# Values behind scores from step 45, and the first keys and queries turned by TensorE: a change to a fused top-k attention and tanh-shrink kernel

## The chip, the cores and the metric

The kernel runs on one core of a Trainium2 chip. Five engines work side by side, each through its own instructions in order: TensorE (PE; its weight loads are listed as PEld), VectorE (DVE), ScalarE (ACT), GpSimd (POOL) and SyncE (SP), which here only issues transfers. Transfers run on 16 DMA engines. The metric is the device time of one launch in microseconds (us).

## The reference

All is float32 except the weights of the second block, which arrive as float64. Eight batches, eight heads, 576 rows, head size 64; then a block over 4608 tokens with 512 features and 2048 hidden ones.

```python
scores = scale * np.matmul(q, k.transpose(0, 1, 3, 2))            # B, H, 576, 576
kth = np.partition(scores, -32, axis=-1)[..., -32:-31]
scores = np.where(scores >= kth, scores, -1000000000.0)
attn = np.exp(scores - np.max(scores, axis=-1, keepdims=True))
attn = attn / (np.sum(attn, axis=-1, keepdims=True) + 1e-09)
x = np.matmul(attn, v)                                            # heads joined: 4608 x 512
h = x @ w_in                                                      # 4608 x 2048
out = (h - np.tanh(h)) @ w_out                                    # 4608 x 512
```

## The kernel before

**Steps.** The work is cut into 144 steps, numbered n in the code and here. A step is 128 query rows (a query tile, `qt` 0 to 3) of a pair of heads (`hp` 0 to 3) of a batch, with all 576 keys; the two heads lie in the two halves of the partitions. Each batch has 16 such steps, and two more (`rem`) that take the last 64 rows of two pairs together. Batch 0 is steps 0 to 17.

**What a step does.** `scores` multiplies queries and keys on PE into one PSUM bank set (`scps`, one buffer) and copies them to SBUF on ACT (`sc`, L244). `search` finds the 32 largest per row on DVE: a minimum and a maximum of the two halves of the keys (L266, L267, the last reads of `scps` by DVE), then four rounds of MAX8 (L274) and three of MATCH_REPLACE8 (L277). Between the rounds stand other DVE jobs: `between(i)` runs what is put down for round i. `mask` builds the threshold on POOL (L293), applies a steep Relu on ACT (L306) and subtracts on POOL, one head after the other (L309). `expo` takes the exponential on ACT (L329). Then the probabilities have to be turned so that keys lie on partitions: in batch 0 by PE against an identity matrix (`turn_pe`, L423, a bank `zt` of two buffers, copied out by ACT, L426), later by DVE in 32x32 blocks (`turn_z`, L386) and two hops of DMA through DRAM (`spread_keys`, L401 and L403). `values` multiplies them with v on PE (L451, the same two-buffer bank, tile `av`) and copies the product to `xT` on ACT (L471); from batch 1 on it comes five steps behind its search.

**The second block.** When all pairs of a unit of 256 (in batch 0 sometimes 128) rows are done, `values` appends the unit's matmuls to the list `work`: L502 into `hps` (evicted by tanh and copy on ACT, L514 and L515, and subtracted on POOL, L516), then L523 into `ops` (copied by ACT, L533, and sent out by SP, L535). `rate` sets a share of that list for each step, and `deal` issues it in parts: 0.4 of a step's share ahead of the scores, 0.6 behind. These are FFN matmuls below.

**The order is written out by hand.** One loop over n issues everything, and each engine runs its instructions in that order. In a step it is: transposes of batch 0's probabilities, `mask(n-1)`, `search(n)`, `spread_keys`, `deal`, `scores(n+1)`, `expo(n-1)`, `deal`, loads, `deal`. `due` issues the values of a step five back. Up to step 44 it stands at the head of the loop; from `NEAR = 45` on it stands between the first `deal` and `scores(n+1)`.

**The start.** All rows of batch 0 are asked for at once, ahead of step 0, with the weights between them, on SP's queue. `load_rows` brings k or q of a pair of heads as four transfers of 32 partitions with runs of 32 floats (128 bytes), so that `turn_rows` can turn them by 32x32 blocks on DVE (L221). Pairs 1 to 3 of batch 0 land in room that later belongs to the weights `w_in[2]` and `w_in[3]` (`early`). Their turns are put down for round 0 of steps 0, 1 and 2: pair 1 in step 0, and so on. The weights are made float32 in 32 pieces of 128 x 512 during steps 0 to 10 (`convert`): two transfers (L148, L149), then DVE (L157, L162), ACT (L160, L165), DVE (L168) and POOL (L171). Pieces 0 to 3 wait behind one load of k and q each in SP's queue. After its last load, v is brought by `load_v` (L211: 128 KB in runs of 256 bytes, L215: 16 KB).

Of the kernel before, what the change touches and what calls it, by code (L numbers as in the profile page):

```python
# [10 lines left out]
FP32 = mybir.dt.float32  # L11
# [8 lines left out]
J = 4  # L20
# [31 lines left out]
def kernel(  # L52
# [9 lines left out]
    nc = tc.nc  # L62
    P = nc.NUM_PARTITIONS
    B, H, S, D = q.shape
    DM, DFF = moe_w_in.shape
    NHP = H // 2
    JP = J * P
    R = S - JP
# [16 lines left out]
    def pool(name, bufs, **kw):  # L85
        return ctx.enter_context(tc.tile_pool(name=name, bufs=bufs, **kw))
# [14 lines left out]
    zt_ps = pool("zt_ps", 2, space=PS)  # L101
    h_ps = pool("h_ps", 2, space=PS)

    ident = consts.tile([P, P], FP32, name="ident")
# [3 lines left out]
    w_in = [consts.tile([P, CD, DFF // WJ], FP32, name=f"w_in{j}") for j in range(WJ)]  # L108
# [14 lines left out]
    def flat(x):  # L123
        return x.rearrange("p n w -> p (n w)")
# [51 lines left out]
    raw, kT, qT, vb, vr = {}, {}, {}, {}, {}  # L176
# [5 lines left out]
    def half(t):  # L182
        return slice(t * D, (t + 1) * D)


    early = [flat(w_in[j][:])[:, i * S : (i + 1) * S] for j in (2, 3) for i in range(3)]

    def load_rows(name, b, hp, exact):

        if b == 0 and hp and not exact:  # L190
            x = early[2 * hp - 2 + (name == "q")]
        else:
            x = ldpool.tile([P, S], FP32, tag=f"{name}in", name=f"{name}in")[:]
        raw[name, b, hp] = x
        src = {"k": k, "q": q}[name]
        for a in range(NG):
            h, d = 2 * hp + a // 2, a % 2 * G
            queue = nc.scalar if a and (name, b, hp, exact) == ("q", 0, 0, False) else nc.sync
            queue.dma_start(  # L199
                x[a * G : (a + 1) * G, :].rearrange("i (n d) -> i n d", d=G),  # L200
                src[b, h, :, d : d + G].rearrange("(n i) d -> i n d", i=G),
            )

    def load_v(b, hp):
# [4 lines left out]
        for t in range(2):  # L209
# [4 lines left out]
            o = 0 if t else JP  # L214
            nc.sync.dma_start(y[half(t), t, :], v[b, h, o : o + R, :])  # L215

    def turn_rows(name, b, hp):

        d = kqpool.tile([P, S], FP32, tag=f"{name}T", name=f"{name}T")
        {"k": kT, "q": qT}[name][b, hp] = d  # L220
        nc.vector.transpose(d[:], raw.pop((name, b, hp)))  # L221

# [2 lines left out]
    def scores(n):  # L227
        g = steps[n]
        ps = sc_ps.tile([P, 2, 2, 512], FP32, tag="sc", name="scps")
        for s in range(2):  # L230
            ks = slice(s * S2, (s + 1) * S2)
            for i in range(2 if g.rem else 1):
                qs = slice(JP, S) if g.rem else slice(g.qt * P, (g.qt + 1) * P)
                rows = half(i) if g.rem else slice(0, P)
                for t in range(2):
                    nc.tensor.matmul(  # L236
                        ps[rows, t, s, 0:S2],
                        qT[g.b, g.hp + i][half(t), qs],
                        kT[g.b, g.hp + i][half(t), ks],
                        start=True,  # L240
                        stop=True,
                    )
        sc = scpool.tile([P, 2, 2, S2], FP32, tag="sc", name="sc")
        nc.scalar.copy(sc[:], ps[:, :, :, 0:S2])  # L244
        st[n] = dict(sc=sc, ps=ps)
# [162 lines left out]
    def turn_pe(n):  # L408

        g, z = steps[n], st.pop(n)["z"]  # L410
        if g.rem:
            et = et_rem
        elif g.i:
            et = ets.pop(n - 1)
        else:
            et = et2[0]
        ets[n] = et
        et = tiles(et, g.nq)[:, :, :, g.i, :].rearrange("p a k j -> p k a j")
        for k0 in range(0, KC, J):
            kn = min(J, KC - k0)  # L420
            zt = zt_ps.tile([P, 512], FP32, tag="zt", name="zt")
            for k in range(kn):
                nc.tensor.transpose(  # L423
                    zt[:, k * P : (k + 1) * P], z[:, (k0 + k) * P : (k0 + k + 1) * P], ident[:]
                )
            nc.scalar.copy(  # L426
                et[:, k0 : k0 + kn],
                zt[:, 0 : kn * P].rearrange("p (k a j) -> p k a j", a=NG, j=G),
            )
            if k0:  # L430
                yield
# [119 lines left out]
    def plan():  # L551
        steps.clear(), done.clear()

        def block(b, qt):
            return [(slice(0, P), out[b * S + qt * P : b * S + (qt + 1) * P, :])]

        rest = None
        for b in range(B):
            if b % 2 == 0:
                rest = Unit(  # L560
                    [[(half(i), out[(b + i) * S + JP : (b + i + 1) * S, :]) for i in range(2)]], "xTr"
                )

            parts = [(0, 1), (2, 3)]
            if b == 0:
                parts[0:1] = [(0,), (1,)]
            for a, qts in enumerate(parts):
                unit = Unit([block(b, qt) for qt in qts], "xT")
                pe = b == 0
                for hp in range(NHP):  # L570
                    for i, qt in enumerate(qts):
                        steps.append(Step(b, hp, qt, unit, 0, i, len(qts), pe))
                    if hp == NHP - 1:
                        done[len(steps) - 1] = unit
                    if hp % 2 and a == (0 if b == B - 1 else len(parts) - 1):
                        steps.append(Step(b, hp - 1, J, rest, b % 2 * R, pe=pe))
                        if hp == NHP - 1 and b % 2:
                            done[len(steps) - 1] = rest
        for g, after in zip(steps, steps[1:]):
            if after.pe and not after.rem and not g.pe:  # L580
                g.lag = 3
# [3 lines left out]

    def run(exact):
        plan()
        NS = len(steps)
        todo, at_round, turned = {}, {}, {}

# [5 lines left out]
        for i, (b, hp) in enumerate(pairs):  # L596
            n = next(n for n, g in enumerate(steps) if (g.b, g.hp) == (b, hp))
# [56 lines left out]
        def here(i):  # L654
            return 0 <= n + i < NS

# [25 lines left out]
        def rate():  # L682


            have, low, high = len(work), 0.0, None
            coming = sorted((t, u.n // 8) for u, t in ready.items() if t > n)
            for t, k in coming + [(NS + LAG, 0)]:
                r = have / max(t - n, 1)
                high = r if high is None else min(high, r)
                have += k  # L690
            for u, t in begun.items():
                if t > n and u in before:
                    need = [i + 1 for i, x in enumerate(work) if x[1] is before[u]]
                    if need:
                        low = max(low, need[-1] / (t - n))
            return max(low, high)
# [3 lines left out]
        def deal(part):  # L700
            nonlocal credit
            credit += part * share
            while work and credit > 0 and work[0][0] <= usable:
                work.pop(0)[2]()
                credit -= 1
            credit = min(credit, 1.0)

        for n in range(-4, NS + LAG):
            pe = here(-2) and steps[n - 2].pe
            def due():  # L710
                for m in (n - LAG, n - LAG + 1, n - LAG + 2):
                    if 0 <= m < NS and steps[m].last and steps[m].lag == n - m:
                        values(m)

            if n < NEAR:
                due()
            share, usable = rate(), converted[0]
            if pe:
                w = turn_pe(n - 2)
                next(w)  # L720
            if here(-1):
                mask(n - 1, exact)
            if here(0):
                search(n, exact, between)
            elif here(-2):
                between(0)
                between(LATE)
            if here(-2) and not pe and steps[n - 2].last:
                spread_keys(n - 2)
            if pe:  # L730
                spread(n - 2)
            deal(0.0 if pe else 0.4)
            if n >= NEAR:
                due()
            if here(1):
                scores(n + 1)
            if pe:
                next(w)
            if here(-1):
                expo(n - 1)  # L740
            deal(0.8 if pe else 0.2)
            if pe and steps[n - 2].last:
                values(n - 2)
            deal(0.0 if pe else 0.2)
            for fn in todo.pop(n, []):
                fn()
            deal(0.2)
# [4 lines left out]
    with tc.manual_schedule():  # L752
        run(False)
# [42 lines left out]
```

## Time and profile before

| what | value |
|---|---|
| median of three runs | 1528.41 us (1525.82 to 1529.62) |
| profiled execution | 1527.48 us, its span 1525.7 us |
| busy PE, DVE, ACT, POOL | 1420.7, 1350.9, 1002.3, 875.1 us |
| granted clock of PE, mean | 0.98 |
| DMA | 221.61 MB, 145 GB/s in the mean |
| chain that ended last, by engine | PE 62%, DVE 26%, ACT 4%, POOL 3% |

The span runs from the first to the last instruction; the 1.8 us between it and the execution's time lie around it. In the page's tenths the span is cut in 40 equal slices of 38 us, and a 9 means 90% busy or more. A row of the timeline has the start, the duration, the engine, the line of the kernel, the operation and its operands, how many it merges, and in brackets how long the engine idled before and what ended that. A row of the waits has who waited for whom, the total in us, how often, and the longest.

### The profile page before, as it was taken

The numbers are of one execution on the slowest core, as the hardware profiler recorded it, in microseconds if no ns is written. First come the engines' busy times: TensorE is split into PE (matmuls) and PEld (weight loads), VectorE is DVE, ScalarE is ACT, GpSimd is POOL, SyncE is SP. The second block draws the span as 40 slices with busy tenths as digits, with TensorE's granted clock in tenths as the row PEclk, the third lists the DMA queues.
The fourth block names the chain that finished last, engine by engine and source line by source line (L and its number), as shares of the span: only waits on it lengthen the run. The fifth ranks groups of instructions, "written<-read, shape, count | busy, mean of one in ns | idle before, by whom it ended". The sixth has DMA issues, their size and how long they took to land.

```text
span 1525.7 us, 24089 instructions
## 1 busy us (share of the span) xinstructions
PE 1420.7 (93%) x7302; PEld 904.1 (59%) x7302; DVE 1350.9 (89%) x3884; ACT 1002.3 (66%) x1801; POOL 875.1 (57%) x1370
## 2 busy tenths in 40 slices
PE   2577898999999999999999999999999999999998
PEld 1355566456565674747574674747475675756673
DVE  7998999999999999999999999999999999887000
ACT  3676677677676776867676776777676776767220
POOL 3788676656474664756555565656464564746110
PEclk9877999999999999999999999999999999999999
DMA  9954214547755676657754675557654676343400
GB/s 255 357 173 164 51 25 108 141 138 175 158 152 165 152 167 155 155 151 166 170 147 131 168 161 151 140 160 160 151 148 131 164 159 165 101 150 113 107 7 17
DMA packets 255467, 221.61 MB, mean 145 GB/s; under 512 B 197728, under 2 KB 204896, under 8 KB 248160
## 3 DMA queue, kind: packets, MB, share of 16 engines
q1 hardware_dynamic: 253552, 219.75, 55.9%
q8 instruction: 60, 0.98, 0.3%
q14 instruction: 79, 0.65, 0.2%
q10 hardware_dynamic: 1776, 0.22, 0.1%
HBM read 136.17 MB, written 83.76 MB: 144 GB/s over the span
## 4 chain that ended last, share of the span: by engine, by line
PE 62%; DVE 26%; ACT 4%; POOL 3%; issue 2%; SPq 1%; DMA 1%; DVEq 0%; ACTq 0%; POOLq 0%
PE hps L502 24%; PE ops L523 24%; PE av L451 7%; DVE m L274 7%; DVE ab L277 7%; PE scps L236 7%; DVE zx L386 3%; DVE ab L267 2%; DVE ab L269 2%; DVE ab L266 2%; SPq L199 1%; DVE f L157 1%; POOL z L309 1%; ACT z L306 1%; DVE f L168 1%
## 5 line engine op out<-in xcount | busy, mean ns | idle before, releaser
L523 PE MATMUL ops<-w_out,g 128*128 128x512 f32 x1152 | 517.7, 600 | 2.1 <-POOL bad L313 1.2
L502 PE MATMUL hps<-xT,w_in 128*128 128x256 f32 (+1 forms) x2176 | 467.2, 372 | 2.5 <-ACT g L515 1.2
L274 DVE MAX8 m<-ab 128x8 f32<-128x288 f32 (+1 forms) x1152 | 467.1, 447 | 0.0
L309 POOL TENSOR_TENSOR z<-sc,z 128x576 f32<-128x576 f32 x288 | 403.0, 1421 | 84.3 <-ACT z L306 84.1
L502 PEld LDWEIGHTS hps<-xT,w_in 128*128 128x128 f32 x2176 | 392.4, 192 | 78.0 <-issue 21.9
L277 DVE MATCH_REPLACE8 ab<-m,ab 128x288 f32<-128x288 f32 x864 | 376.2, 443 | 0.0
L523 PEld LDWEIGHTS ops<-w_out,g 128*128 128x128 f32 x1152 | 213.3, 191 | 262.5 <-issue 248.6
L306 ACT ACTIVATE z<-sc,tb 128x576 f32<-128x576 f32 x288 | 207.7, 769 | 146.4 <-POOL tb L293 131.6
L516 POOL TENSOR_TENSOR g<-g,th 128x512 f32<-128x512 f32 x144 | 183.2, 1273 | 147.1 <-ACT g L515 142.1
L355 ACT ACTIVATE z<-z,rd 128x576 f32<-128x576 f32 x252 | 180.8, 764 | 101.6 <-DVE rd L348 101.5
L236 PE MATMUL scps<-kT,qT 64*128 64x288 f32 (+1 forms) x1280 | 190.6, 449 | 44.8 <-DVE qT L221 27.2
L329 ACT ACTIVATE z<-z,nb 128x576 f32<-128x576 f32 x288 | 221.6, 775 | 2.5 <-POOL z L309 2.4
L339 POOL TENSOR_SCALAR rd<-den 128x2 f32<-128x2 f32 x144 | 33.4, 232 | 327.7 <-ACT z L329 323.7
L244 ACT COPY sc<-scps 128x1152 f32<-128x1152 f32 x144 | 160.5, 1114 | 41.3 <-PE scps L236 41.1
L386 DVE STREAM_TRANSPOSE zx<-z 128x1152 f32<-128x1152 f32 x126 | 171.9, 1364 | 16.2 <-ACT z L355 16.1
L236 PEld LDWEIGHTS scps<-kT,qT 64*128 64x128 f32 (+1 forms) x1280 | 103.6, 185 | 122.5 <-issue 49.9
L266 DVE TENSOR_TENSOR ab<-scps,sc 128x576 f32<-128x576 f32 x144 | 105.3, 731 | 28.9 <-ACT sc L244 24.0
L514 ACT ACTIVATE th<-hps 128x512 f32<-128x512 f32 x144 | 84.3, 585 | 64.4 <-PE hps L502 62.0
L269 DVE MAX8 ab<-ab 128x8 f32<-128x288 f32 x288 | 115.8, 443 | 0.0
L267 DVE TENSOR_TENSOR ab<-scps,sc 128x576 f32<-128x576 f32 x144 | 107.1, 744 | 0.0
L451 PE MATMUL av<-et,vb 128*64 128x256 f32 (+1 forms) x640 | 76.2, 371 | 17.6 <-ACT et L426 17.6
L293 POOL TENSOR_SCALAR tb<-m 128x1 f32<-128x1 f32 x288 | 88.4, 316 | 6.9
(68 smaller groups left out, 1067.7 us busy)
## 6 DMA issues: line engine op xcount, KB each, us to landing
there<-zx SPq DMA_DIRECT2D x56, 1152.0 KB, 4.2
spare<-there SPq DMA_DIRECT2D x112, 288.0 KB, 5.4
et<-there SPq DMA_DIRECT2D x112, 288.0 KB, 5.2
kin<-in_k_dram SPq DMA_DIRECT2D x116, 72.0 KB, 2.9
vb<-in_v_dram SPq DMA_DIRECT2D x64, 128.0 KB, 6.2
out_dram<-ot SPq DMA_DIRECT2D x32, 256.0 KB, 4.3
qin<-in_q_dram SPq DMA_DIRECT2D x113, 72.0 KB, 3.6
there<-zx SPq DMA_DIRECT2D x14, 576.0 KB, 5.0
```

The costliest lines, as they stand in the source:

```text
L236: nc.tensor.matmul(ps[rows, t, s, 0:S2], qT[g.b, g.hp + i][half(t), qs], kT[g.b, g.hp + i][half(t), ks], start=True, stop=True,)
L274: nc.vector.max(m[:, t, m8], last[t] if i == rounds - 1 else cur[t])
L277: nc.vector.match_replace(nxt[t], m[:, t, m8], cur[t], NEG)
L306: nc.scalar.activation(zv[:, t, :], scf[:, t, :], AF.Relu, bias=tb[:, t : t + 1], scale=-BIG)
L309: nc.gpsimd.tensor_tensor(zv[:, t, :], scf[:, t, :], zv[:, t, :], ALU.subtract)
L329: nc.scalar.activation(x["zv"][:, t, :], x["zv"][:, t, :], AF.Exp, bias=x["nb"][:, t : t + 1], scale=scale, accum_out=den[:, t : t + 1],)
L355: nc.scalar.activation(x, x, AF.Copy, scale=rds[n][:, g.i, t : t + 1])
L386: nc.vector.transpose(tiles(zx, g.nq)[:, :, :, g.i, :].rearrange("p c k j -> p k c j"), z[:].rearrange("p (k c j) -> p k c j", c=NG, j=G),)
L451: nc.tensor.matmul(av[half(t), 0, cols], vb[g.b, hp][:, t, c, :] if c < J else vr[g.b, hp][:, t, :], es[:, :, (J + 1) * t + c if c < J els ...
L502: nc.tensor.matmul(cur[u][:, s : s + w], w_in[j][:, c, fo : fo + P], u.xT[:, c, 0:w], start=(c == 0), stop=(c == CD - 1),)
L516: nc.gpsimd.tensor_tensor(g, g, th[:], ALU.subtract)
L523: nc.tensor.matmul(cur[u][:], u.g[o // 1024][:, o % 1024 // 512, o % 512 : o % 512 + P], w_out[f // FJ][:, f % FJ, :], start=(f == 0), sto ...
```

## The change

It has two parts.

For pairs 1 to 3 of batch 0, `load_rows` brings rows to partitions as they stand: row p of a block of 128 goes to partition p, with both heads' 64 floats side by side, so a load is two transfers of 512 runs and two of 64 runs of 256 bytes. A region of `early` grows from 576 to 640 columns. `turn_rows` turns such a block by PE transposes against the identity (four of 128 x 128 into one `zt` buffer, one of 64 rows into the other), and ACT copies each buffer to `kT` or `qT`. The place in the order stays: round 0 of steps 0, 1 and 2. The second pass (`exact`), which runs only when a flag at the end asks for it, keeps DVE's turns.

From step 45 on, `scores(n+1)` is issued ahead of `due`, so that the values of a step follow the scores instead of preceding them.

```diff
-    early = [flat(w_in[j][:])[:, i * S : (i + 1) * S] for j in (2, 3) for i in range(3)]
+    early = [flat(w_in[j][:])[:, 5 * i * P : 5 * (i + 1) * P] for j in (2, 3) for i in range(3)]
...
+        if b == 0 and hp and not exact:
+
+            xv = x.rearrange("p (c t d) -> p t c d", t=2, d=D)
+            for t in range(2):
+                h = 2 * hp + t
+                nc.sync.dma_start(
+                    xv[:, t, 0:J, :], src[b, h, 0:JP, :].rearrange("(c p) d -> p c d", p=P)
+                )
+                nc.sync.dma_start(xv[0:R, t, J, :], src[b, h, JP:S, :])
+            return
...
+    turned_pe = [True]
+
     def turn_rows(name, b, hp):

         d = kqpool.tile([P, S], FP32, tag=f"{name}T", name=f"{name}T")
         {"k": kT, "q": qT}[name][b, hp] = d
-        nc.vector.transpose(d[:], raw.pop((name, b, hp)))
+        x = raw.pop((name, b, hp))
+        if not (b == 0 and hp and turned_pe[0]):
+            nc.vector.transpose(d[:], x)
+            return
+        for c0, c1, w in ((0, J, P), (J, J + 1, R)):
+            zt = zt_ps.tile([P, 512], FP32, tag="zt", name="zt")
+            for c in range(c0, c1):
+                o = (c - c0) * P
+                nc.tensor.transpose(zt[:, o : o + w], x[0:w, c * P : (c + 1) * P], ident[0:w, 0:w])
+            w = (c1 - c0 - 1) * P + w
+            nc.scalar.copy(d[:, c0 * P : c0 * P + w], zt[:, 0:w])
...
         plan()
+        turned_pe[0] = not exact
...
             deal(0.0 if pe else 0.4)
+            if here(1):
+                scores(n + 1)
             if n >= NEAR:
                 due()
-            if here(1):
-                scores(n + 1)
             if pe:
                 next(w)
```

## The prediction

> **What bounds the kernel now.** I read the page's busy tenths first, then the chain of waits, then PE's waits alone, then the timeline at the two places that the change touches. The page and the chain:
>
> ```profile
> PE   2577898999999999999999999999999999999998
> ...
> DVE  7998999999999999999999999999999999887000
> ...
> PE 62%; DVE 26%; ACT 4%; POOL 3%; issue 2%; SPq 1%; DMA 1%; DVEq 0%; ACTq 0%; POOLq 0%
> ```
>
> Two bounds in turn: DVE while PE is still at 2 to 8 tenths, PE afterwards. Stretches of the timeline in windows and PE's waits after 430 us say where it turns (columns of a window: length, then busy time of PE, PEld, DVE, ACT, POOL):
>
> ```profile
> 0.00:430.00 430.00, 339.25 (x1883) 221.82 (x1884) 407.68 (x1162) 291.64 (x531) 275.95 (x422) 0.94 0.58 159
> 430.00:660.00 230.00, 226.36 (x1161) 142.39 (x1161) 228.32 (x665) 164.96 (x295) 140.74 (x228) 1.00 0.63 156
> 660.00:912.00 252.00, 249.89 (x1306) 159.77 (x1302) 246.54 (x712) 179.16 (x321) 149.21 (x239) 1.00 0.65 158
> 912.00:1411.50 499.50, 498.59 (x2509) 312.56 (x2509) 464.94 (x1345) 346.61 (x619) 293.02 (x468) 1.00 0.57 145
> ...
> PE scps L236 <- DVE ab L267: 2.3, 2, 1.2
> PE ops L523 <- POOL bad L313: 1.2, 1, 1.2
> PE hps L502 <- ACT ot L533: 1.1, 1, 1.1
> PE ops L523 <- POOL rd L339: 0.9, 1, 0.9
> PE hps L502 <- ACT g L515: 0.9, 1, 0.9
> ```
>
> PE idles 90.8 us before 430, and 3.6 + 2.1 + 0.9 = 6.6 us from there to 1411. So after 430 no reordering can gain more than about 6.6 us; the start has more, but there DVE is busy almost throughout, and only DVE work or a wait of DVE counts.
>
> **The loads.** Six loads (k and q of pairs 1 to 3) keep 24 issues on SP, but 2304 packets of 128 B become 1152 of 256 B each; bytes are the same (0.295 MB a load). In the DMA view of the first 40 us, in slices of 1 us, those that lie between the weights' peaks show 115 to 158 GB/s, about 140, so 2.1 us a load; between 40 and 70 us, where v comes in 256 B packets among the weights, no slice but the last is under 276 GB/s, so at most 1.1 us. Piece 3 of the weights, behind all six, lands up to 6 us earlier; the other end is nothing. SP's four issues take 2.8 to 3.4 us now and 2.8 to 3.3 for a load of v (0.38 to 0.60 and 0.47 to 1.90 us): no change. On the path lies one wait of DVE: 0.85 us at 31.27.
>
> **The turns.** Six DVE transposes go, two in each of steps 0, 1, 2. In step 1:
>
> ```profile
> 25.11 2.77 POOL L309 TENSOR_TENSOR z<-sc,z 128x576 f32<-128x576 f32 x2 [0.41 <-ACT z L306]
> ...
> 26.06 0.77 DVE L221 STREAM_TRANSPOSE kT<-w_in 128x576 f32<-128x576 f32 x1
> ...
> 26.75 0.74 DVE L221 STREAM_TRANSPOSE qT<-w_in 128x576 f32<-128x576 f32 x1
> ...
> 27.41 0.75 DVE L157 TENSOR_SCALAR f<-w_out 128x512 uint32<-128x512 uint32 x1
> ...
> 31.27 0.43 DVE L162 TENSOR_SCALAR w_in<-w_out 128x512 uint32<-128x512 uint32 x1 [0.85 <-DMA w_out<-in_moe_w_in_dram]
> ```
>
> From 26.06 to 27.41 they take 1.35 us; three pairs, 4.1 us. But L157 behind them needs 0.43 us elsewhere (30.00) and 0.75 here: it ends 0.28 us after POOL's subtraction (25.11 + 2.77). In step 2 the same: started at 40.10, it took 1.18. The turns stand where DVE would be held anyway. So in steps 1 and 2 the gain lies between 0 (L157 still waits for POOL's second subtraction) and 1.35 us (it slips in ahead of it). Without turns L157 comes 1.35 us sooner, during POOL's first subtraction. The nearest row for that case:
>
> ```profile
> 91.35 3.24 POOL L309 TENSOR_TENSOR z<-sc,z 128x576 f32<-128x576 f32 x2
> ...
> 92.57 0.74 DVE L168 SCALAR_TENSOR_TENSOR f<-w_out,f 128x512 uint32<-128x512 uint32 x1
> ...
> 93.24 1.63 DVE L157 TENSOR_SCALAR f<-spare 128x512 uint32<-128x512 uint32 x1
> ```
>
> Here DVE came during the first of the two, ran in 0.74 us, and POOL's pair took 3.24 instead of 2.77: DVE got in between, POOL paid 0.47. I take 1.35 for both steps. (At 44.44 L157 and L162 ran back to back while POOL's L171 took 1.65 instead of 1.27, so L162 should follow through the same gap.)
>
> The Trainium skill, page "SBUF — State Buffer", section "Who interferes with whom", has a rule that speaks against the gain: VectorE in a two-port mode and GpSimd share one port pair, and whoever issues first holds it for the whole instruction while the other fully blocks. The held L157 agrees (0.28 us behind POOL's end). If POOL's second subtraction counts as issued first, steps 1 and 2 gain nothing by it, and the sum below would be 2.7 us smaller; the row at 92.57 speaks for the gap.
>
> With 2.7 us of lead DVE reaches L162 of piece 3 at 30.43 - 2.7 = 27.7; if piece 3 lands 3.5 us earlier or more (of up to 6) the 0.85 us wait goes too. I take it. Lead after step 2: 3 x 1.35 + 0.85 = 4.9 us, ends 1.35 and 4.9.
>
> In exchange PE gets 30 transposes (eight take 1.97 us at 34.19, so about 1.2 us a tensor) and ACT 12 copies (0.59 us for 512 columns; 64 columns cost 0.21 as xTr's copy, so 0.8 a tensor, 4.9 us in all). They wait for the load and for a bank of two that the copy frees. Behind them on PE stand the scores of step n+1; on ACT the conversions L160 and L165, then the scores' copy. In step 2 the turns' copies follow L306 (37.37 + 1.44 = 38.8); two tensors' worth with a bank's wait is about 2.5 us, until 41.3, and ACT now idles until 41.31 for L157. Score copies: at 46.03 for a search at 48.62. So ACT and PE have cover (PE is busy 2.0 to 5.7 of each 10 us up to 50); without it, the 4.9 us of ACT would come onto DVE's path.
>
> Behind step 2 the program is as before up to step 45, and DVE waits on engines that wait on DVE: I let the lead through to 430 whole. The clock is a doubt (0.66 to 0.69 granted between 60 and 90 us), 1 us either way.
>
> **Values behind scores.** The values' matmuls take 2.31 us (1.32 for the rest rows), the scores' 1.17. No DMA and no POOL instruction is moved; on PE the two swap, on ACT the xT copy goes behind the scores' copy. FFN matmuls keep their places. The values now end where the scores ended; ACT's exponentials behind them then wait for a copy of 0.37 us instead of 1.1, so no later than before. Three units (FFN from 608.2, 1291.4, 1364.3) start right behind their last values; the scores no longer cover the xT copy there. At 324.9, where nothing covers it, PE lost 0.15 us: 0.5 in all, within the ends below. Where PE is the bound and the score bank is long free, nothing changes: same work, same order of the rest. It costs where PE comes to the scores just as DVE frees the bank:
>
> ```profile
> 577.31 1.95 PE L451 MATMUL av<-et,vb 128*64 128x256 f32 x16
> ...
> 579.62 1.24 PE L236 MATMUL scps<-kT,qT 64*128 64x288 f32 x8
> 580.79 3.70 PE L523 MATMUL ops<-w_out,g 128*128 128x512 f32 x8
> 584.42 0.69 PE L451 MATMUL av<-spare,vb 128*64 128x64 f32 x16
> ...
> 586.95 1.24 PE L236 MATMUL scps<-kT,qT 64*128 64x288 f32 x8 [1.14 <-DVE ab L267]
> ```
>
> Followed row by row with the new order: scores 577.5, values to 579.8 + FFN to 583.4, idle 3.5 until 586.95 (L267 ends 586.80), rest values to 589.4, FFN 7.13 to 596.6, scores, FFN to 604.8; there the values that stood ahead (604.74) no longer cover the bank's 605.3, idle 0.5, scores, values to 608.8 where FFN went on at 608.2: 0.6 us lost. At 921 the same reckoning (bank free 922.2, rest values 1.32 moved behind) gives 0.4. Elsewhere scores start 2 to 6 us after L267. What it can gain: DVE is fed earlier in a values step, but DVE's waits for the scores' copy (20.9 us) lie after 960, where PE is the bound. I take +1.0 us; ends -6.6 (all of PE's idle) and +3 (five places like 586).
>
> **Sum.** -4.9 + 1.0 = -3.9 us. The profiled execution is 1527.48 us (span 1525.7 and 1.8 around it), 0.9 below the median of 1528.41; the difference is taken off the median: 1524.5 us.
>
> **Rivals.** *POOL holds DVE* (steps 1 and 2 gain nothing): lead 1.35 to 2.2, less 1.0: 1527.2 to 1528.1. For it, L157's 0.28; against it, 92.57. *Order pays too*: of the 6.6 us half is won, 4.9 + 3.3: 1520.2. Against it, the waits for POOL and ACT there (506, 764, 788, 912) end on work whose place doesn't change. *Values lose their cover (slower)*: some 58 value groups follow 430 us (46 copies of xT, 24 half ones of xTr). If PE finds the bank busy at the scores so often that 0.17 us is lost on average, that is 9.9 us, against a lead of 4.9: 1533.4; it decides from 0.085 us each. For it, PE already waits 1.14 and 1.18 at 586 and 596; against it, the 2 to 6 us elsewhere. *Lead lost on the way*: from search to search steps 7 to 10 last 13.6 to 16.4 us, on ACT, POOL and PE; if the lead vanishes there, +1.0: 1529.4.
>
> **How the numbers follow.** 0.3% is 4.6 us, about what a measurement of this kernel can tell. Forecast 0.55 (1522 to 1527; 0.22 of it beyond 4.6 us), POOL holds 0.15, order pays 0.13, cover lost 0.12 (0.10 beyond), lead lost 0.05. Faster 0.22 + 0.13 = 0.35, slower 0.10, same 0.55. The range 1519.5 to 1530.5 leaves out the lost cover and tails of the rest.
>
> **What would show it.** After: the search of step 3 starts near 43.7 instead of 48.62; POOL's L309 near 24 and 35 us stretched by 0.4 to 1.4 while L157 stays at 0.4; L162's wait gone; PE's idle before 430 smaller by about 4.9; waits of scores for L267 after 470 grown by about 1 us beyond the 2.3, DVE's for the scores' copy shrunk without effect. I am wrong if L157 still ends 0.28 behind POOL in steps 1 and 2, if DVE now waits for ACT's score copy in steps 1 to 3, or if PE's idle after 470 changes by more than 3 us.

## The result: 1526.6 us against 1529.0

The changed kernel took 1526.55 us in the median of four executions (1523.93 to 1528.46), the kernel before 1529.01 us beside it: a ratio of 0.9985, interval 0.9961 to 1.0009, too little to tell from no change. Twelve more executions beside 23 of the kernel before (experiment e10) gave 1526.59 against 1528.08 us in the medians, ratio 0.9988, interval 0.9979 to 0.9997. Two of the twelve, at 1691 and 8220 us, were slow runs and are left out of the ratio. The interval just leaves out 1, so there is a gain, of about 1.8 us (0.0012 x 1528; 0.5 to 3.2 by the interval), not the 3.9 us forecast. The profiled execution took 1525.3 us, its span 1523.5 us, 2.2 us less than before.

The page's busy tenths of PE and DVE and its chain of waits, after:

```profile
PE   4567898999999999999999999999999999999998
...
DVE  7998999999999999999999999999999999887000
...
PE 56%; DVE 33%; ACT 4%; POOL 2%; issue 2%; DMA 1%; SPq 0%; DVEq 0%; ACTq 0%; POOLq 0%
```

The bounds are the same two. PE's first tenth grew from 2 to 4 (the transposes), DVE's are unchanged: it is busy 1349.5 us, before 1350.9. The stretches of the timeline that were shown of before, moved with the searches (length, busy time of PE, PEld, DVE, ACT, POOL, then the granted clock, DMA share and GB/s):

```profile
0.00:427.30 427.30, 348.41 (x1913) 227.80 (x1914) 405.96 (x1156) 295.17 (x543) 273.87 (x422) 0.92 0.58 161
427.30:657.30 230.00, 225.85 (x1157) 142.06 (x1155) 227.78 (x662) 164.36 (x294) 140.46 (x227) 1.00 0.62 153
657.30:909.30 252.00, 249.88 (x1307) 160.01 (x1308) 246.47 (x713) 178.63 (x319) 149.46 (x240) 1.00 0.66 158
909.30:1408.80 499.50, 498.22 (x2508) 312.32 (x2507) 465.86 (x1345) 346.03 (x621) 292.00 (x468) 1.00 0.57 145
```

PE idles 78.9 us in the first stretch instead of 90.8. Only some 2.7 us of that are the stretch being shorter; the rest is mostly PE's transposes (six tensors at 1.4 us), which is added work and no gain. PE's waits from 427 us on, after (who waits for whom: us in total, times, longest):

```profile
PE scps L258 <- DVE ab L289: 3.3, 4, 2.3
PE ops L545 <- POOL bad L335: 1.2, 1, 1.2
PE hps L524 <- ACT ot L555: 1.0, 1, 1.0
PE ops L545 <- POOL rd L361: 0.9, 1, 0.9
PE hps L524 <- ACT g L537: 0.9, 1, 0.9
```

Only the first line moved: the scores wait 3.3 us for DVE instead of 2.3. (Behind `turn_rows`, line numbers are 22 higher than before: scores L258, their copy L266, the search's first two passes L288 and L289, POOL's subtraction L331. L157 to L171 keep theirs.)

The most telling number is the start of each step's search, since DVE sets the pace of the start and PE that of the rest. The table gives it for before, and for the others the difference (minus is earlier); it holds the experiments too, and the text returns to it.

| search of step | 1 | 2 | 3 | 5 | 7 | 8 | 16 | 45 | 66 | 100 | 142 |
|---|---|---|---|---|---|---|---|---|---|---|---|
| before, us | 22.4 | 35.1 | 48.6 | 73.8 | 99.3 | 114.7 | 203.8 | 464.5 | 657.1 | 975.1 | 1383.3 |
| after | -1.1 | -2.2 | -2.3 | -3.1 | -3.1 | -2.8 | -2.8 | -2.7 | -2.2 | -1.7 | -1.7 |
| e10: after again | -1.0 | -2.1 | -2.2 | -3.0 | -3.0 | -2.8 | -1.7 | -1.7 | -1.1 | -0.6 | -0.5 |
| e1: first part alone | -1.2 | -2.3 | -2.4 | -3.2 | -3.2 | -4.5 | -4.6 | -4.6 | -4.6 | -4.6 | -4.6 |
| e2: order alone | -0.1 | +0.7 | +0.7 | +0.7 | +0.7 | -0.6 | -0.7 | -0.7 | -0.1 | +0.3 | +0.4 |
| e7: order, five steps spared | -0.2 | +0.5 | +0.5 | +0.5 | +0.5 | +0.9 | +0.9 | +0.9 | +0.8 | +0.9 | +0.9 |
| e4: e1, pieces later | -1.3 | -3.7 | -5.1 | -5.1 | -5.1 | -5.0 | -3.8 | -3.8 | -3.8 | -3.8 | -3.8 |
| e5: before, pieces later | 0.0 | -0.1 | -0.7 | 0.0 | 0.0 | +0.4 | +1.3 | +1.3 | +1.3 | +1.3 | +1.3 |
| e6: e4, steps 3 to 9 too | -1.2 | -3.3 | -4.7 | -4.1 | -5.2 | -5.3 | -4.6 | -4.6 | -4.6 | -4.6 | -4.6 |
| e3: 128-byte runs | +1.6 | +5.2 | +5.0 | +5.0 | +5.0 | +6.3 | +7.6 | +7.6 | +7.6 | +7.6 | +7.6 |
| e8: e4, three issues a load | -1.3 | -3.8 | -5.2 | -5.2 | -5.3 | -5.2 | -3.9 | -3.9 | -3.9 | -3.9 | -3.9 |
| e9: e4, two issues a load | +0.5 | -2.1 | -3.5 | -3.5 | -3.5 | -3.1 | -3.3 | -3.3 | -3.3 | -3.3 | -3.3 |

Step 0 became 1.0 us shorter (from its search to the next), step 1 1.1, step 2 only 0.15. The timeline of steps 1 and 2, after, shows why (start, us, engine, line, operation):

```profile
15.94 0.43 DVE L162 TENSOR_SCALAR w_in<-w_out 128x512 uint32<-128x512 uint32 x1 [0.22 <-DMA w_out<-in_moe_w_in_dram]
...
24.02 2.94 POOL L331 TENSOR_TENSOR z<-sc,z 128x576 f32<-128x576 f32 x2 [0.41 <-ACT z L328]
...
24.98 0.73 DVE L157 TENSOR_SCALAR f<-w_out 128x512 uint32<-128x512 uint32 x1
...
25.63 1.62 DVE L162 TENSOR_SCALAR w_in<-w_out 128x512 uint32<-128x512 uint32 x1
...
29.08 0.41 DVE L162 TENSOR_SCALAR w_in<-w_out 128x512 uint32<-128x512 uint32 x1
...
36.03 2.94 POOL L331 TENSOR_TENSOR z<-sc,z 128x576 f32<-128x576 f32 x2 [0.41 <-ACT z L328]
...
36.55 1.17 DVE L157 TENSOR_SCALAR f<-spare 128x512 uint32<-128x512 uint32 x1
...
37.64 1.62 DVE L162 TENSOR_SCALAR w_in<-spare 128x512 uint32<-128x512 uint32 x1
```

POOL's row holds two subtractions. L157 gets in between them, as forecast: POOL's pair took 2.94 us instead of 2.77. But L162, which takes 0.41 us elsewhere (29.08), then takes 1.62 us: it ends at 27.25, 0.29 us after POOL's second subtraction (24.02 + 2.94). In step 2 the same, 0.29 us after POOL again. The two engines alternate here, and DVE ends its pair of instructions nearly where it ended before, with turns or without: 5.89 us behind the start of the search in step 1 (before 6.05) and 6.34 in step 2 (before 6.49). This is what the Trainium skill, page "SBUF — State Buffer", section "Who interferes with whom", says of the port pair that VectorE and GpSimd share: an exclusive lock for the whole instruction. These rows add where waiting DVE got its turn: between two instructions of POOL.

Step 1's 1.1 us are L162's wait for its transfer, gone at 29.08 (it now starts 0.33 us behind its L157, before 1.27), and the 0.16 us by which the held pair ended sooner; step 2 has only the latter. Step 0 gave 1.0 instead of 1.35, because a new wait for the transfer came in: L162 (15.94) starts 0.64 us behind its L157, before 0.30.

### The profile page after: what moved, and what is told of

Same layout as the page of the kernel before. It is cut to its first block, busy times and chain, and to the rows that moved or that the text cites. A ratio compares the mean times of both kernels' runs of the same rounds, so it can differ in the third digit from the quotient of the medians.

```text
span 1523.5 us, 24155 instructions
## 1 busy us (share of the span) xinstructions
PE 1430.0 (94%) x7332; PEld 910.3 (60%) x7332; DVE 1349.5 (89%) x3878; ACT 1004.4 (66%) x1813; POOL 873.0 (57%) x1370
## 4 chain that ended last, share of the span: by engine, by line
PE 56%; DVE 33%; ACT 4%; POOL 2%; issue 2%; DMA 1%; SPq 0%; DVEq 0%; ACTq 0%; POOLq 0%
PE hps L524 22%; PE ops L545 21%; DVE m L296 9%; DVE ab L299 9%; PE av L473 7%; PE scps L258 6%; DVE zx L408 4%; DVE ab L291 3%; DVE ab L289 3%; DVE ab L288 3%; DVE f L157 1%; DVE f L168 1%; ACT z L328 1%; ACT sc L266 1%; ACT z L377 1%
## 5 line engine op out<-in xcount | busy, mean ns | idle before, releaser
L331 POOL TENSOR_TENSOR z<-sc,z 128x576 f32<-128x576 f32 x288 | 403.2, 1422 | 89.6 <-ACT z L328 89.6
L258 PE MATMUL scps<-kT,qT 64*128 64x288 f32 (+1 forms) x1280 | 190.4, 449 | 27.9 <-DVE ab L289 17.2
L266 ACT COPY sc<-scps 128x1152 f32<-128x1152 f32 x144 | 160.0, 1111 | 37.6 <-PE scps L258 37.6
L258 PEld LDWEIGHTS scps<-kT,qT 64*128 64x128 f32 (+1 forms) x1280 | 103.5, 185 | 116.4 <-issue 38.9
L288 DVE TENSOR_TENSOR ab<-scps,sc 128x576 f32<-128x576 f32 x144 | 104.9, 729 | 20.9 <-ACT sc L266 15.6
L289 DVE TENSOR_TENSOR ab<-scps,sc 128x576 f32<-128x576 f32 x144 | 106.9, 742 | 0.0
L473 PE MATMUL av<-et,vb 128*64 128x256 f32 (+1 forms) x640 | 75.8, 370 | 15.8 <-ACT et L448 15.8
L315 POOL TENSOR_SCALAR tb<-m 128x1 f32<-128x1 f32 x288 | 86.3, 309 | 6.9
```

The source lines that it names most:

```text
L258: nc.tensor.matmul(ps[rows, t, s, 0:S2], qT[g.b, g.hp + i][half(t), qs], kT[g.b, g.hp + i][half(t), ks], start=True, stop=True,)
L331: nc.gpsimd.tensor_tensor(zv[:, t, :], scf[:, t, :], zv[:, t, :], ALU.subtract)
L473: nc.tensor.matmul(av[half(t), 0, cols], vb[g.b, hp][:, t, c, :] if c < J else vr[g.b, hp][:, t, :], es[:, :, (J + 1) * t + c if c < J els ...
```

## The experiments

In the expectations, H is the theory that I held when the run was put down; each says there what it claims.

### The two parts alone (e1, e2), and the changed kernel once more (e10)

e1 is the change without its last hunk; e2 is that hunk alone:

```diff
             deal(0.0 if pe else 0.4)
+            if here(1):
+                scores(n + 1)
             if n >= NEAR:
                 due()
-            if here(1):
-                scores(n + 1)
```

> The loads and turns of the change alone; values stand ahead of the scores as before. Theory H (held): the lead of the changed kernel comes from the first pair of turns and from weights that land earlier (2.3 us at the search of step 3, 2.7 us from there to step 45), and the order costs 1.0 us later. Then the search of step 3 starts near 46.3 us (before: 48.6), PE's waits for L267 after 470 us are 2.3 us as before, and the span is 1.0 us shorter than the changed kernel's 1523.5: about 1522.5, 0.998 of before. Rival N (the order is neutral): the span is that of the changed kernel, 1523.5. Rival P (the order pays): it is longer, 1524 or more.

> Values behind the scores from step 45 on, and nothing else. Theory H: steps 0 to 57 keep their times; PE waits for L267 at the scores of steps 59, 61 and 95 grow from 2.3 to about 3.3 us, so the search of step 66 and all behind it start 0.6 us later and PE's end lies 1.0 us later: span about 1526.7, ratio 1.0007. Rival N: no difference beyond 0.3 us in PE's waits. Rival P: PE's idle after 470 us falls and the span is 2 to 3 us shorter, 0.998.

e1: 1524.48 against 1528.38 us, ratio 0.9977 (0.9968 to 0.9986), so 3.5 us faster (2.1 to 4.9). Its profile's span is 1520.6 us, 1.9 less than expected; that came behind step 7 (last section). e2: ratio 1.0008 (0.9999 to 1.0017), 1.2 us slower, within what can't be told from nothing. The table tells more. e1 keeps its lead from step 45 to 142 to within 0.1 us; e2, which before step 45 is the kernel before, loses 0.6 us between steps 65 and 66 (-0.7 to -0.1) and 0.4 to step 100, and otherwise less than 0.1. PE's waits of e2 for the scores' bank, in the timeline of PE:

```profile
586.23 1.24 PE L236 MATMUL scps<-kT,qT 64*128 64x288 f32 x8 [2.31 <-DVE ab L267]
...
604.54 1.24 PE L236 MATMUL scps<-kT,qT 64*128 64x288 f32 x8 [0.45 <-DVE ab L267]
605.71 1.95 PE L451 MATMUL av<-spare,vb 128*64 128x256 f32 x16
```

Before, the first of these was 1.14 and stood with a second one of 1.18 at 595.3: their 2.32 is the 2.31 here, and the 0.45 is new. The forecast had followed just these rows. (Its idle of 3.5 us leaves out the scores' own 1.17; the row shows 2.31. The sum is not touched, since the bank's time set where the row ended.)

> The changed kernel as it stands, for more rounds and a second profile. Theory H (the start gives 2 to 4.5 us, depending on the clock that PE is granted between 90 and 180 us, the order costs 1.0 to 1.1): median 1.0 to 1.2 us above that of e1 against the same before, a ratio of 0.9983 to 0.9987; the searches 0.6 us later at 66 against 65 and 0.4 later at 100, and the lead at step 7 within 0.4 us of the first profile's 3.1, that at 16 anywhere from 2.7 to 4.6. Rival (the lead is the program's, 2.7 at step 16): 2.6 to 2.9 there again.

e10 gave 0.9988; it should have been 0.9983 to 0.9987. The order's two losses are there again in the table (0.6 at step 66, 0.4 at 100), and the first seven steps agree with the first profile to 0.1 us. Then the same program lost 1.2 us between steps 9 and 16 that it had not lost in the first profile: a lead of 1.7 at step 16, less than either theory allowed.

### Where the order costs (e7)

```diff
+            first = n >= NEAR and n not in (57, 58, 60, 93, 94)
+            if here(1) and first:
+                scores(n + 1)
             if n >= NEAR:
                 due()
-            if here(1):
+            if here(1) and not first:
                 scores(n + 1)
```

> The new order alone from step 45 (e2), except in steps 57, 58, 60, 93 and 94, where the old order stays; turns and loads as before. Theory H (the order costs only at these places, where PE comes to the scores just as VectorE frees the bank): PE's waits of the scores for L267 after 430 us back at 2.3 to 2.6 us (e2: 3.4), PE's idle time after 430 at 6.5 to 6.8, lead of the searches unchanged between steps 45 and 142 within 0.2 us, time within 1 us of before. Rival (every values step costs a little, by the order itself): the searches still lose 1.0 us between 45 and 142. Rival 2 (the order pays elsewhere): they gain over 0.3 us.

PE's first wait after 430 us in e7:

```profile
PE scps L236 <- DVE ab L267: 2.5, 3, 1.2
```

With the old order in five of 99 steps the scores' waits are back at 2.5 us, and the searches keep their distance from step 45 to 142 to within 0.1 us (0.8 to 0.9). So the order's cost of 1.0 to 1.1 us is in those five steps, and the order neither costs nor gains anywhere else. The time itself, ratio 1.0006 (0.9997 to 1.0015), can't tell e7 from e2: this profile had come to step 45 0.9 us later than before, with the same program.

### The held L162 (e4, e5, e6)

e4 is e1 with the pieces' instructions of steps 1 and 2 issued a round later, behind POOL's subtractions; no instruction is added or taken away. The list gives the round of each part of a piece (L157 with L162, or L168), in order:

```diff
+            where = {1: (1, 1, 2, 3), 2: (1, 1, 2, 2, 3, 3)}.get(m) or [3 * i // max(len(seq) - 1, 1) for i in range(len(seq))]
+            for r, x in zip(where, seq):
+                at_round.setdefault((m, r), []).append(lambda x=x: part(*x))
-            for i, x in enumerate(seq):
-                at_round.setdefault((m, 3 * i // max(len(seq) - 1, 1)), []).append(
-                    lambda x=x: part(*x)
-                )
```

> As e1_turns_only, and the weights' DVE work L157 and L162 of steps 1 and 2 is moved from round 0 of the search to round 1 (in step 2 some L168 to rounds 2 and 3), so that it comes when POOL's subtraction L309 of that step is over. Theory H: L157 and L162 stood in POOL's way there (0.73 and 1.62 us instead of 0.42), so the two steps become about 1.3 us shorter each: the search of step 3 starts near 43.7 to 44.3, piece 3 (landing at 28.2) just in time, and the whole is 2 to 2.7 us shorter than e1_turns_only. Rival C (DVE gained all three pairs of turns and the copies of the turns on ACT took 2 us back): ACT's conversions come later still, the search of step 3 starts at 46.3 or later.

e4's timeline around the two places:

```profile
23.77 2.78 POOL L331 TENSOR_TENSOR z<-sc,z 128x576 f32<-128x576 f32 x2 [0.41 <-ACT z L328]
...
26.29 0.54 DVE L157 TENSOR_SCALAR f<-w_out 128x512 uint32<-128x512 uint32 x1
...
26.75 0.41 DVE L162 TENSOR_SCALAR w_in<-w_out 128x512 uint32<-128x512 uint32 x1
...
34.58 2.77 POOL L331 TENSOR_TENSOR z<-sc,z 128x576 f32<-128x576 f32 x2 [0.41 <-ACT z L328]
...
36.73 0.90 DVE L157 TENSOR_SCALAR f<-spare 128x512 uint32<-128x512 uint32 x1
...
37.55 0.41 DVE L162 TENSOR_SCALAR w_in<-spare 128x512 uint32<-128x512 uint32 x1
...
43.53 0.76 DVE L288 TENSOR_TENSOR ab<-scps,sc 128x576 f32<-128x576 f32 x1
```

DVE now spends those 2.8 us on the next round of its search. L162 is back at 0.41 us, POOL's pair at 2.77, and the search of step 3 starts at 43.53, the 43.7 that was forecast for the change itself: 2.6 us earlier than in e1. Steps 1 and 2 last 10.37 and 12.07 us, in e1 11.58 and 13.33: 1.2 and 1.3 us shorter, close to the 1.35 of a pair of turns that the change did not get. (The remaining 0.2 came in step 0, where piece 1 landed sooner.) The time is 1523.21 us, ratio 0.9966 (0.9952 to 0.9979), the fastest version here together with e8. Against e1 it is 1.7 us (0.0011 x 1528) with intervals that overlap, so the times alone don't show it. Nor do the ends of the two profiles: 1.3 us came to e1 between steps 7 and 8 (last section), and from step 16 on e1 is ahead by 0.8 us.

> The kernel before, with VectorE's turns, old loads and old order, but L157 and L162 of the pieces of steps 1 and 2 moved behind POOL's two subtractions, as in e4. Theory H (VectorE could not have done pieces there while GpSimd subtracts, the turns are a filler of that time): only the held part of L157 comes back, 0.33 us in step 1 (0.75 instead of 0.42) and 0.76 in step 2 (1.18), so the search of step 3 starts about 1.1 us earlier than before, 47.0 to 48.0, and the turns and the pieces together are worth more (5.1 in e4) than each alone (2.4 in e1, about 1.1 here). Rival (place of the pieces is worth 2.7 us by itself, as between e1 and e4): 45.9 and a time 2.7 us under before. Rival 2 (turns ahead of pieces were no filler, and moving the pieces costs ACT's start): 48.6 or later.

e5 applies the same move to the kernel before: ratio 1.0001 (0.9992 to 1.0011). The search of step 3 starts 0.7 us earlier than before, within theory H's 47.0 to 48.0 but less than its 1.1, and nothing of it is left at step 5. In step 1 the freed 0.33 us went into another wait, of L162 for its transfer, which had been 0.85 us at 31.27. Step 2 gave 0.6. Step 3 then lost 0.7 to a wait for ACT that the kernel before does not have there. DVE's two lines in e5:

```profile
31.18 0.43 DVE L162 TENSOR_SCALAR w_in<-w_out 128x512 uint32<-128x512 uint32 x1 [1.16 <-DMA w_out<-in_moe_w_in_dram]
...
55.23 0.69 DVE L168 SCALAR_TENSOR_TENSOR f<-w_out,e 128x512 uint32<-128x512 uint32 x1 [0.61 <-ACT e L160]
```

So the turns were a filler: before, they stood in time in which DVE couldn't have done the pieces anyway. Step 2, in which DVE waits for no transfer, shows it best. It lasts 13.50 us before, 13.35 with the turns gone (after), 12.89 with the pieces moved (e5) and 12.07 with both (e4): 0.15 and 0.6 us alone, 1.4 together. In the other profiles of the same arrangement these lengths come again to 0.03 us (e2 and e7; e1 and e10; e6, e8 and e9); e5 alone has no second profile.

e6 moves the third piece of steps 3 to 9 as well, which is held for 1.26 instead of 0.42 us at 51.44 in e4:

```diff
-            where = {1: (1, 1, 2, 3), 2: (1, 1, 2, 2, 3, 3)}.get(m) or [3 * i // max(len(seq) - 1, 1) for i in range(len(seq))]
+            where = ({1: (1, 1, 2, 3), 2: (1, 1, 2, 2, 3, 3)} | {m: (0, 0, 1, 2, 2, 3) for m in range(3, 10)}).get(m) or [3 * i // max(len(seq) - 1, 1) for i in range(len(seq))]
```

> e4, and in steps 3 to 9 the third L157 and L162 of each step, which stand in the time of POOL's subtraction (1.26 us instead of 0.42 at 51.44 in e4), go behind it. Theory H (only the hold costs): 0.84 us a step, up to 5.9 us over seven steps, of which a part goes to the wait of VectorE for ACT's conversion that stands there already (0.61 us at 50.83); I expect the search of step 7 1.5 to 3 us ahead of e4's and 1.5 to 4 us at step 13, the time 1519 to 1522. Rival (VectorE then waits for ACT at L168 instead, by as much): step 7 within 0.5 us of e4's 94.1, the wait ahead of L168 grown from 0.6 to 1.4 us, the time 1523. Rival 2 (the lead of the start is given back to a lower granted clock between 92 and 150 us): step 7 ahead as H says, step 13 not.

1522.99 us, ratio 0.9975 (0.9966 to 0.9984), and the search of step 7 at 94.1 as in e4. The rival's number came true, but not by its mechanism: DVE's wait for ACT stayed at 0.62 us. The piece left one hold and met the next, in e6's timeline of step 3:

```profile
53.29 1.27 POOL L171 TENSOR_TENSOR w_in<-w_in,f 128x512 f32<-128x512 f32 x1
53.38 1.47 DVE L157 TENSOR_SCALAR f<-w_out 128x512 uint32<-128x512 uint32 x1
```

L157 came 0.09 us after POOL's L171 and ended 0.29 us after it. POOL is busy for 10.7 of the 13.3 us of this step, so a place for a piece has to be found, not only another place.

### What sets when the pieces land (e3, e8, e9)

The forecast took a load from 2.1 to at most 1.1 us and piece 3 up to 6 us earlier. The second transfer of pieces 1, 2 and 3 landed at 16.93, 24.38 and 31.25 us before and at 15.91, 22.25 and 28.21 after: 7.2 and 6.15 us apart, two loads of k and q and one piece each time, so 0.5 us a load and 3.0 us at piece 3. (In e2 and e7, the same start as before, piece 3 landed at 31.94 and 31.73; by those it is up to 0.75 us a load and 3.7 us.)

e3 halves the runs of e1, to the 128 bytes that they had before the change, which takes two more issues a load:

```diff
+                for e in range(2):
+                    de = slice(e * G, (e + 1) * G)
-                nc.sync.dma_start(
-                    xv[:, t, 0:J, :], src[b, h, 0:JP, :].rearrange("(c p) d -> p c d", p=P)
-                )
+                    nc.sync.dma_start(
+                        xv[:, t, 0:J, de], src[b, h, 0:JP, de].rearrange("(c p) d -> p c d", p=P)
+                    )
                 nc.sync.dma_start(xv[0:R, t, J, :], src[b, h, JP:S, :])
```

> As e1_turns_only, but the 512 runs of 256 bytes of each transfer are loaded as two transfers of 512 runs of 128 bytes: the same rows to the same places in nearly as many packets as before the change (2176 a load instead of 1152). Theory H: the loads' share of the lead is gone, because piece 1 of the weights lands again near 16.9 and piece 3 near 31.3 us and DVE waits for both; the search of step 3 starts at 48 or later, the lead is under 0.7 us. Rival L (length of the runs doesn't matter, only the turns do): 46.3 as in e1_turns_only.

Measured: 1534.51 us (one execution), the search of step 3 at 53.6, pieces 8.9 us apart (18.56, 27.63, 36.43). The loads matter more than the theory allowed: 5.0 us lost at step 3 with DVE's turns gone as in e1. But e3 changed two things, the run's length and the issues, so e8 and e9 changed the issues alone, at 256 bytes. e8, on e4, makes one transfer of the two heads' last 64 rows; e9, on e8, puts that one on ACT's queue (`nc.scalar`). The edit of e8:

```diff
             for t in range(2):
                 h = 2 * hp + t
                 nc.sync.dma_start(
                     xv[:, t, 0:J, :], src[b, h, 0:JP, :].rearrange("(c p) d -> p c d", p=P)
                 )
-                nc.sync.dma_start(xv[0:R, t, J, :], src[b, h, JP:S, :])
+            nc.sync.dma_start(
+                xv[0:R, :, J, :], src[b, 2 * hp : 2 * hp + 2, JP:S, :].rearrange("t p d -> p t d")
+            )
```

> e4 with the two 64-row transfers of a load made one, so three issues a load instead of four; runs of 256 bytes as in e4. Theory H (SP's issues, back to back at 0.4 to 0.6 us and eight of them between two pieces of the weights, set when pieces land, not the transfers): landing of the second transfer of pieces 1, 2 and 3 comes 5.0 to 5.2 us apart instead of 6.2, piece 3 near 25 us instead of 28. Rival (the transfers' own rate limits): still 6.0 to 6.3 apart. Either way VectorE waits for no piece in steps 1 and 2 in e4, so the time stays within 1.5 us of e4's 1523.2 and the search of step 3 within 0.7 us of 43.5.

> As e8, with that one transfer on ACT's queue: SP issues two per load, four between two pieces. Theory H (SP's issues limit): pieces land 3.5 to 4.5 us apart, where the transfers themselves (1.6 MB at the 400 GB/s that the trace shows at its best) take over as the limit, piece 3 near 21 to 23 us. Rival (the transfers' rate limits already): 6 us apart. ACT's six issues stand ahead of its first copies and may push step 0 back by up to 1 us. Time within 1.5 us of e4's.

With four, three and two issues a load on SP the pieces land 6.0 (e4), 5.7 and 4.9 us apart; theory H had said 6.2, 5.1 and 4.0 or so, the rival 6 throughout. Neither holds. Fewer issues help by 0.3 and 0.8 us, less than the two issues of about 0.55 us that each step saves between two pieces, because the others get longer. SP's rows in e9 and in e4 for the same issue, the first transfer of piece 1:

```profile
10.00 2.09 SPq L148 DMA_DIRECT2D w_out<-in_moe_w_in_dram  x1
```

```profile
10.07 0.54 SPq L148 DMA_DIRECT2D w_out<-in_moe_w_in_dram  x1
```

What held SP in that row no view shows. Two loads and a piece (1.64 MB) in 4.9 us are 334 GB/s, where the trace shows 400 to 430 at its best. There is a third limit that neither theory had. SP's waits of the changed kernel in the first 27 us have this line:

```profile
SPq L204 <- DMA w_out<-in_moe_w_in_dram: 2.2, 3, 0.8
```

Each of the three waits ended as the second transfer of a piece landed, the one issued eight issues before (landings at 9.50, 15.91 and 22.25, issues at 9.52, 15.93 and 22.26). In the trace the issues wait on eight semaphores in turn, so no more than eight transfers are under way at once. So the number of issues counts (e8, e9), and something else limits too; the shares of the transfers' rate and of this wait were not separated. The times, 0.9962 (0.9947 to 0.9976) for e8 and 0.9977 (0.9968 to 0.9986) for e9, fit the searches: e8 is as e4, since e4 waited only 0.2 us for a piece there; e9 loses 1.0 us at step 0 (piece 0 issued at 6.7 instead of 3.7) and is 1.6 us behind e4 at step 3.

## Why the prediction was right and wrong

**The outcome.** No change that can be told in one measurement, and a time inside the range, were right, but the range of 11 us also holds a kernel without any gain. The likeliest time was 2 us too low, and the mechanism behind 2.7 of its 4.9 us of lead was wrong.

**The turns: the step that failed.** The forecast took 1.35 us for each of steps 1 and 2, "by row 92.57", and added that "L162 should follow through the same gap", from a place (44.44) where POOL ran its L171. L157 did find the gap; L162 did not: 1.62 us, to 0.29 behind POOL's second subtraction, twice. So in steps 1 and 2 the turns gained 0.15 to 0.2 us, next to the lower end of nothing that the forecast had named, and the rival *POOL holds DVE* was right on the mechanism. The row at 92.57 showed the fault already: behind it L157 stands at 93.24 with 1.63 us. It is the second of two DVE instructions, it was held by POOL's second subtraction, and it was left out of the reckoning. At 44.44 DVE's first was already running when POOL's L171 came (44.66); in steps 1 and 2 POOL was there first. e4 shows that the price itself was nearly right: 2.5 us for the two pairs (1.2 and 1.3), once DVE had something else to do.

**The loads: right in direction, off in size.** Forecast: a load to 1.1 us or less, a gain of 1.0 us; measured 0.5 to 0.75. SP's issues count too, as e8 and e9 show; the forecast had set them down as "no change" and so as no limit. That they take as long as before is right; that they then help to bound the rate was missed, and so was SP's wait for a landing. What was taken from it, the wait of 0.85 us, did go. Piece 1 came too late by 0.22 us for step 0's full gain.

**The lead.** 4.9 us were forecast after step 2 (ends 1.35 and 4.9); 2.3 us were measured (3.0 and 2.8 against the starts of e2 and e7, where DVE waited 0.6 to 0.7 us more for pieces). A further 0.7 us came in step 4, which the forecast had not counted: before, DVE waited 0.62 us for ACT's conversion at 68.13, after it did not. The lengths of the steps sort the profiles: step 4 lasts 12.9 us in the five with 128-byte runs (before, e2, e3, e5, e7) and 12.2 in the others (e6: 12.4); step 3 lasts 12.9 to 13.3 us in the five with the pieces moved (e4, e5, e6, e8, e9) and 12.2 in the others. So the loads (e3 against e1) and the place of the pieces (e4 against e1) move this wait; by what path was not followed.

**ACT and PE have cover** held: DVE waits for no score copy in steps 1 to 3. Each tensor's transposes take 1.4 us on PE and 0.7 us on ACT, and the scores follow them.

**The lead goes through to 430 whole, the clock 1 us either way: too narrow.** The last section has the numbers. From step 16 to 45 it did go through, to within 0.1 us in every run.

**Values behind the scores: right, in size and place.** +1.0 forecast, 0.6 at 577 to 608 and 0.4 at 921; measured 0.6 and 0.4, in those steps and only there (e2, e7). *Values lose their cover* didn't happen; *Order pays too* neither, since the waits for POOL and ACT at 506, 764, 788 and 912 are the same to 0.1 us in every kernel.

**The sum**, by its own steps with measured terms: -2.3 (step 3) - 0.7 (step 4) + 1.1 (order) = -1.9, where -1.8 was measured (e10's ratio). That the two meet is partly luck: by its profiles the changed kernel's start varies by 1.1 us behind step 7.

## What to carry to other kernels

When an instruction goes from an engine, ask what that engine would have done in its place: if the next one needs a resource that another engine holds until then, the removed work was a filler, and only a second change, which puts other work there, brings the gain out (in step 2 here 0.15 and 0.6 us alone, 1.4 together). When a row is used as a precedent for a gap, read the row behind it too: the first instruction through a gap says nothing of the second. And a few us near the start of a kernel are best compared step by step up to the first place where the profiles of one program differ among themselves, not by the end.

## What the runs showed of the hardware

**The start of one program repeats up to step 7, and then it doesn't.** The steps up to 45 are the same program in e1, after and e10, and their searches agree to 0.2 us up to step 7. From there they part: leads of 4.6, 2.8 and 1.7 us at step 16. The kernel before, e2 and e7 are one program up to step 45, too. Their steps 0 to 6 have the same lengths to 0.03 us but for step 1, where DVE waits for pieces 2 and 3 to land (12.7, 13.5 and 13.4 us); at step 16 they stand at 0, -0.7 and +0.9. In step 7 the granted clock shows it. The windows of e1 (columns: length, busy time of PE, PEld, DVE, ACT, POOL, then the granted clock, DMA share and GB/s):

```profile
98.00:101.00 3.00, 3.00 (x27) 2.83 (x28) 3.00 (x11) 0.88 (x3) 2.92 (x5) 1.00 0.90 329
```

and of after:

```profile
98.00:101.00 3.00, 3.00 (x15) 3.00 (x16) 3.00 (x11) 0.37 (x1) 2.92 (x5) 0.50 0.93 364
```

The second block's matmuls that stand there took 1.95 us in e1 (from 98.02) and 3.41 us in after (from 98.20), and batch 0's transposes of the probabilities, behind them on PE, came 1.6 us later. ACT's Relu and conversions stand behind their copies: the search of step 8 came 1.7 us later in after. In the kernel before the matmuls took 3.13 us (from 101.30) and DVE waited 2.02 us for ACT ahead of its L168; in e2 they took 1.95 us (from 101.90) and DVE waited 0.73. The work is the same and DVE is the bound there, yet 3 us of a halved clock on PE reach it through ACT.

All twelve profiles bear this out. Their clock falls to 0.50 in stretches of 3.4 us or a multiple of it, at different times in each, and the length of a step goes by the stretches that begin in its first 10 us:

| stretches at half clock | step 7, us | step 9, us |
|---|---|---|
| none | 14.1, 14.2 (e1, e2) | 15.5 (e2, e7, e9), 15.2 (e6) |
| one of 3.4 us | 15.3 to 15.8 (nine others) | 16.1 to 16.9 (seven others) |
| one of 6.8 us | 16.7 (e3) | 17.2 (e5) |

Step 12 begins 1 to 3 us behind such a stretch and lasts 9.4 to 9.5 us where that one was 3.4 us long (before, e1, e5), 9.8 to 10.3 where it was 6.8. The other steps from 7 to 16 have the same length in every profile to 0.1 us, but for e6, whose order differs there. So a lead at step 16 tells little of a change of 1 us, and the lengths of steps 2 to 6 tell a good deal. What sets the place of the stretches was not tried.

**DVE gets in between two instructions of POOL; the reverse is no rule.** L157 and L162 take 0.41 us alone, 0.73 and 1.17 when they come during POOL's first subtraction and 1.62 during the second. Both L162 of the changed kernel, e6's L157 and e4's two L157 (0.54 and 0.90 us) end 0.28 or 0.29 us behind the end of POOL's row, whenever they had come. But where DVE came first, POOL did not get in between DVE's two, in the changed kernel's timeline:

```profile
42.09 0.41 DVE L157 TENSOR_SCALAR f<-zx 128x512 uint32<-128x512 uint32 x1
42.31 1.66 POOL L171 TENSOR_TENSOR w_in<-w_in,f 128x512 f32<-128x512 f32 x1 [2.22 <-DVE f L168]
42.42 0.41 DVE L162 TENSOR_SCALAR w_in<-zx 128x512 uint32<-128x512 uint32 x1
```

L171 takes 1.27 us elsewhere, so it was held for 0.39 us, until L162 was nearly done. Beside four of these DVE instructions in a row, at 49.45, POOL's two small L315 took 1.90 us instead of 0.56. What decides who goes next was not tried.

**Short transfers are slow by their issue, too.** A load of 0.295 MB costs SP about 0.55 us for each transfer whatever its size (16 KB and 128 KB alike), and where SP had fewer of them to issue, single issues stretched to 2.09 and 2.47 us (e9, the first transfers of pieces 1 and 2).
